# Unused matrix products of 64 columns in place of 128, in a kernel whose order is planned ahead

## The chip, the cores and the metric

The kernel runs on one core of one Trainium2 chip. The metric is device time in microseconds, the median of repeated executions; lower is better. A core has a matrix engine (PE, with its weight loads shown apart as PEld), two elementwise engines that read the matrix engine's results (DVE and ACT), a third that does not (POOL), and a queue that issues DMA transfers (SP).

## The reference

Attention over 4 batches, 8 heads, 576 tokens, 64 features a head, then two feed-forward layers over the 2304 tokens:

```python
scores = scale * np.matmul(q, k.transpose(0, 1, 3, 2))
thresh = np.max(scores, axis=-1, keepdims=True) - tau
scores = np.where(scores >= thresh, scores, -1000000000.0)
attn = softmax(scores);  x = np.matmul(attn, v)      # to [2304, 512]
h = x @ w_in                                          # 512 -> 2048
g = np.where(h >= 1, h, np.where(h <= -1, 0.0, (h + 1) ** 2 / 4))
x = g @ w_out                                         # 2048 -> 512
h = x @ w_in2;  r = np.maximum(h, 0.0)
out = (s * (r * r) + b) @ w_out2
```

All inputs and the result are float32.

## The kernel before, in words

Attention goes through 32 units (batch, half of the query rows, pair of heads). For a block of 128 query rows of a head, PE makes the scores (lines 583 and 592), DVE takes the row's extreme (line 638), ACT the exponentials (641), DVE masks and sums (646), one of three engines normalizes (676, 681), PE transposes the result (702, 718), ACT or DVE copies it out of the matrix engine's result banks (694), and PE multiplies it with the values (740, 741). Beside the first units, parts of the first feed-forward layer run (935 hidden products, 968 output products; 1016 is its remainder after attention). The other half of that layer and the second layer follow in three passes over three blocks of 768 tokens (lines 1230, 1270, 1306), with weights split into two parts and some products combined so that fewer are needed.

The order of the instructions on every engine is fixed when the program is written. Each step is a `Task` with a priority, the engines that could do it and a cost in nanoseconds; `Sched.run` simulates the engines with these costs and with fixed hand-over times between engines (`HOP`), and gives every free engine the ready task of the best priority. The instructions are then written in the order of the planned starts. Result banks are part of the plan: a task group gets a bank when one is free in the plan.

One rule concerns the matrix engine alone. Whenever it has nothing ready in the plan, before 200 us of planned time (`FILL`), and one of the banks 7, 6, 5, 4 is free, `Sched.run` puts in a product that nobody reads: `fill`, line 1406, identity times identity, written to that bank. In the plan it occupies the matrix engine for `fill_ns`, 213.0, plus a change cost between kinds of work (`CHANGE`), and holds the bank for that time; then the engine looks for ready work again. So a gap of the plan holds as many such products as are needed to cover it. The plan also models the matrix engine's clock (`Array`), in which these products count as work. Products planned before 4.5 us (`FILL_FROM`) are not written out. The program's warm-up (line 788) is five products of the same form.

Of the kernel before, what the change touches and what calls it, by code (L numbers as in the profile page):

```python
# [37 lines left out]
FILL = 200000.0  # L38
# [328 lines left out]
def attention_then_ffn(tc, qk, v, tau, w1, w2, s2, b2, out):  # L367
    nc = tc.nc
    sch = Sched()
# [18 lines left out]
    ident = lp.tile([128, 128], F32, name="ident")  # L388
# [51 lines left out]
    bank = [ps2[i][:, x, :] for i in range(2) for x in range(2)] + [t[:, :] for t in ps1] + [ps3[:, x, :] for x in range(2)]  # L440
# [962 lines left out]
        gemm2(P, t0, T)  # L1403

    def fill(b):
        return lambda: nc.tensor.matmul(bank[b][:, 0:128], ident, ident, start=True, stop=True)

    sch.fill_until, sch.fill_banks, sch.fill_ns, sch.fill = FILL, (7, 6, 5, 4), 213.0, fill
    order = sch.run()
    with tc.manual_schedule():  # L1410
        for t in order:
# [70 lines left out]
```

## Time and profile before

| | us |
|---|---|
| median of 3 runs | 1068.74 |
| lowest, highest | 1066.87, 1070.09 |
| the profiled execution, its own time | 1070.16 |
| its span, first to last instruction | 1068.4 |

| engine | busy us | share of the span | instructions |
|---|---|---|---|
| PE | 1044.9 | 98% | 6464 |
| PEld | 924.2 | 86% | 6464 |
| DVE | 802.4 | 75% | 1585 |
| ACT | 708.3 | 66% | 1325 |
| POOL | 434.5 | 41% | 660 |

Busy time is the time in which at least one instruction of the engine runs. Instructions of PE overlap, so a group's busy time is less than count times mean. An entry "idle before" is the time in which the engine did nothing ahead of an instruction, with the instruction that released it. PEclk is the granted share of the matrix engine's full clock of 2.4 GHz; 0.50 is 1.2 GHz.

### The profile page before, as it was taken

What the parts mean: (1) busy time and instruction counts of PE and PEld (TensorE: products, weight loads), DVE (VectorE), ACT (ScalarE), POOL (GpSimd) and SP (SyncE); (2) the same over time, 40 slices, a digit from 0 to 9 for tenths busy, and PEclk for the clock granted to TensorE, in tenths of its full rate; (3) what the DMA queues carried; (4) which work ended last, traced back from release to release, by engine and by line L of the source; (5) the groups of instructions that cost most, each with busy time, mean ns of one, the idle gap of its engine ahead of it and who ended that gap; (6) DMA issues with size and microseconds to landing.
All of it is one profiled execution on the core that took longest, in us unless ns stands there. A gap on an engine that the chain in (4) does not pass through costs nothing.

```text
span 1068.4 us, 19016 instructions
## 1 busy us (share of the span) xinstructions
PE 1044.9 (98%) x6464; PEld 924.2 (86%) x6464; DVE 802.4 (75%) x1585; ACT 708.3 (66%) x1325; POOL 434.5 (41%) x660
## 2 busy tenths in 40 slices
PE   8989999999999999999999999999999999999998
PEld 5556867788888988889999999998988989898996
DVE  7978998788787888857897988787696826446372
ACT  7988888989998988844544636367495735437260
POOL 5766767889798887623212202120111100010000
PEclk9989999999999999999999999999999999999999
DMA  5644465565656664599956579863539943230112
GB/s 179 197 145 145 141 185 186 182 183 172 189 158 213 189 207 155 172 313 373 350 173 218 167 255 387 295 221 138 174 112 306 373 140 118 77 101 20 60 30 89
DMA packets 105120, 199.95 MB, mean 187 GB/s; under 512 B 11328, under 2 KB 33344, under 8 KB 105024
## 3 DMA queue, kind: packets, MB, share of 16 engines
q1 hardware_dynamic: 105024, 198.75, 56.3%
q8 instruction: 51, 0.84, 0.3%
q14 instruction: 45, 0.37, 0.1%
HBM read 134.61 MB, written 64.09 MB: 186 GB/s over the span
## 4 chain that ended last, share of the span: by engine, by line
PE 71%; ACT 7%; DVE 5%; POOL 3%; issue 2%; DMA 1%; DVEq 0%; POOLq 0%; ACTq 0%; SPq 0%
PE ps L1230 24%; PE ps L1306 18%; PE ps L1270 9%; PE ps L935 5%; PE ps L968 4%; PE ps L702 2%; PE ps L740 2%; PE ps L1016 2%; ACT p L681 2%; PE ps L592 2%; DVE p L646 1%; ACT e L641 1%; ACT pt L694 1%; PE ps L583 1%; POOL lr L561 1%
## 5 line engine op out<-in xcount | busy, mean ns | idle before, releaser
L1230 PE MATMUL ps<-pr,lr 128*128 128x384 f32 x816 | 144.2, 334 | 0.0
L1230 PEld LDWEIGHTS ps<-pr,lr 128*128 128x128 f32 x816 | 141.6, 188 | 0.0
L646 DVE SCALAR_TENSOR_TENSOR p<-ps,stt,e 128x576 f32<-128x576 f32 x144 | 116.3, 812 | 22.9 <-ACT e L641 16.7
L1230 PE MATMUL ps<-lr 128*128 128x384 f32 x672 | 121.2, 334 | 0.1
L638 DVE TENSOR_REDUCE stt<-ps 128x1 f32<-128x576 f32 x144 | 105.8, 749 | 17.8 <-PE ps L592 9.3
L1230 PEld LDWEIGHTS ps<-lr 128*128 128x128 f32 x672 | 117.0, 188 | 0.9 <-DVE pf L1135 0.5
L935 PE MATMUL ps<-xh,lr 128*128 128x320 f32 (+1 forms) x512 | 112.5, 299 | 0.3 <-DVE lf L945 0.2
L641 ACT ACTIVATE e<-ps,stt 128x576 f32<-128x576 f32 x144 | 105.7, 749 | 8.6 <-DVE stt L638 8.1
L681 ACT ACTIVATE p<-p,stt 128x576 f32<-128x576 f32 (+3 forms) x112 | 93.2, 837 | 13.3 <-DVE stt L665 12.1
L562 DVE TENSOR_TENSOR pr<-lg,pr 128x768 fp32r<-128x768 f32 x71 | 70.9, 1004 | 39.5 <-POOL pr L845 25.9
L1306 PE MATMUL ps<-lr,pr 128*128 128x512 f32 x432 | 99.1, 390 | 0.0
L1306 PEld LDWEIGHTS ps<-lr,pr 128*128 128x128 f32 x432 | 81.0, 188 | 16.6
L1134 ACT COPY lg<-ps 128x384 f32<-128x384 f32 (+1 forms) x113 | 55.4, 493 | 60.3 <-PE ps L1230 41.6
L702 PE MATMUL ps<-ident,p 128*128 128x128 f32 x576 | 83.2, 276 | 7.5 <-ACT pt L694 5.3
L935 PEld LDWEIGHTS ps<-xh,lr 128*128 128x128 f32 x512 | 85.1, 188 | 3.2 <-DVE lf L945 0.9
L968 PE MATMUL ps<-g,lr 128*128 128x256 f32 (+1 forms) x600 | 87.2, 297 | 0.0
L1138 DVE TENSOR_TENSOR lg<-lg,ps 128x384 f32<-128x384 f32 (+1 forms) x104 | 57.2, 561 | 37.0 <-PE ps L1306 19.3
L702 PEld LDWEIGHTS ps<-ident,p 128*128 128x128 f32 x576 | 66.2, 141 | 20.3 <-ACT pt L694 5.9
L694 ACT COPY pt<-ps 128x512 f32<-128x512 f32 x143 | 79.8, 590 | 5.5 <-PE ps L702 5.1
L968 PEld LDWEIGHTS ps<-g,lr 128*128 128x128 f32 x600 | 80.7, 189 | 0.0
L935 PE MATMUL ps<-xl,lr 128*128 128x256 f32 (+1 forms) x256 | 75.3, 294 | 0.0
L845 POOL CAST pr<-lf 128x768 fp32r<-128x768 f32 x6 | 5.0, 831 | 166.8 <-PE ps L1306 116.6
(127 smaller groups left out, 2335.2 us busy)
## 6 DMA issues: line engine op xcount, KB each, us to landing
wd<-lh SPq DMA_DIRECT2D x118, 256.0 KB, 3.9
lr<-wd SPq DMA_DIRECT2D x108, 256.0 KB, 5.7
lk<-in_w_dram SPq DMA_DIRECT2D x48, 512.0 KB, 4.7
vr<-in_v_dram SPq DMA_DIRECT2D x32, 320.0 KB, 3.4
r<-in_qk_dram SPq DMA_DIRECT2D x32, 288.0 KB, 3.0
lg<-y1T SPq DMA_DIRECT2D x6, 1536.0 KB, 6.8
lk<-in_w_dram SPq DMA_DIRECT2D x32, 256.0 KB, 3.7
r<-in_qk_dram SPq DMA_DIRECT2D x16, 304.0 KB, 4.4
```

The source lines that it names most:

```text
L562: ("dve", dve_ns(n), lambda: nc.vector.tensor_tensor(out=o(), in0=x(), in1=y(), op=op), True)]
L638: add([("dve", 665, lambda: nc.vector.tensor_reduce(out=nm[:, x:x + 1], in_=Sv(), axis=AX.XY, op=ALU.min))], at(pr, "min"), r=[kg], w=[ks[ ...
L641: add([("act", 624, lambda: nc.scalar.activation(out=ev, in_=Sv(), func=AF.Exp, bias=nm[:, x:x + 1], scale=-1.0))], at(pr, "exp"), r=[kg, ...
L646: nc.vector.scalar_tensor_tensor(out=p[:, x * S:x * S + S].rearrange("p (a c) -> p a c", a=2), in0=Sv(), scalar=nthr[:, x:x + 1], in1=ev, ...
L681: nc.scalar.activation(out=p[i:j, o:o + w], in_=p[i:j, a:a + w], func=AF.Identity, scale=rc[i:j, x:x + 1], bias=un[i:j, x:x + 1])
L694: add([("act", actp_ns(n), lambda: [nc.scalar.copy(out=a, in_=b) for a, b in zip(dst, src())]), ("dve", dve_ns(n), lambda: [nc.vector.tens ...
L702: nc.tensor.transpose(bank[g.banks[0]][:, j * 128:(j + 1) * 128], p[:, c0 + j * 128:c0 + (j + 1) * 128], ident)
L935: nc.tensor.matmul(o, a, x, start=(n == 0), stop=(n == 11))
L968: nc.tensor.matmul(o, a[:, c], x, start=(f == 0 and n == 0), stop=(f == nf - 1 and n == 2))
L1230: nc.tensor.matmul(o, a, y, start=(i == 0 and p in (1, 5, 2)), stop=(i == 5), skip_group_check=p not in (1, 5, 2))
L1270: nc.tensor.matmul(o, w, x, start=(f == rows[0] and s == 0), stop=(f == rows[-1] and s == 2))
L1306: nc.tensor.matmul(o, a, y, start=(f == rows[0] and s == 0), stop=(f == rows[-1] and s == 2))
```

## The change

The unused product keeps its stationary operand, the whole 128x128 identity, and streams 64 columns of it in place of 128. Its planned cost is 107 ns in place of 213. As the planner uses this cost, it draws a new order for the whole program.

```diff
     def fill(b):
-        return lambda: nc.tensor.matmul(bank[b][:, 0:128], ident, ident, start=True, stop=True)
+        return lambda: nc.tensor.matmul(bank[b][:, 0:64], ident, ident[:, 0:64], start=True, stop=True)

-    sch.fill_until, sch.fill_banks, sch.fill_ns, sch.fill = FILL, (7, 6, 5, 4), 213.0, fill
+    sch.fill_until, sch.fill_banks, sch.fill_ns, sch.fill = FILL, (7, 6, 5, 4), 107.0, fill
```

## Rows read from the trace of the kernel before

**Rows 1.** The page, busy time of each engine.

```profile
PE 1044.9 (98%) x6464; PEld 924.2 (86%) x6464; DVE 802.4 (75%) x1585; ACT 708.3 (66%) x1325; POOL 434.5 (41%) x660
```

**Rows 2.** Stretches: start and end, length, busy us (instructions) of each engine, clock.

```profile
core 0: us, PE busy (x) PEld busy (x) DVE busy (x) ACT busy (x) POOL busy (x), PEclk, DMA share, GB/s
...
20.00:34.00 14.00, 13.80 (x95) 8.33 (x93) 13.32 (x39) 13.60 (x28) 9.00 (x20) 1.00 0.53 159
...
66.48:73.31 6.83, 6.62 (x28) 3.16 (x29) 4.79 (x13) 5.88 (x14) 2.63 (x7) 0.50 0.33 99
...
137.00:150.00 13.00, 12.69 (x98) 9.72 (x98) 12.70 (x37) 12.66 (x30) 7.04 (x15) 1.00 0.68 207
...
205.00:500.00 295.00, 287.14 (x2133) 257.57 (x2130) 233.35 (x542) 240.20 (x493) 221.55 (x309) 1.00 0.65 208
500.00:900.00 400.00, 399.61 (x2182) 382.11 (x2181) 307.07 (x472) 216.91 (x352) 61.67 (x66) 1.00 0.68 235
900.00:1066.50 166.50, 164.48 (x815) 147.16 (x814) 84.89 (x120) 73.48 (x106) 9.35 (x11) 1.00 0.18 60
```

**Rows 3.** Lines 1406 and 788: durations in ns (least/median/most), first and last start.

```profile
L1406 PEld LDWEIGHTS ps<-ident x94: 186/192/333, 5.2 to 149.4; 128*128 128x128 f32 x94
L1406 PE MATMUL ps<-ident x94: 272/275/579, 5.2 to 149.6; 128*128 128x128 f32 x94
...
L788 PE MATMUL ps<-ident x10: 421/421/582, 1.3 to 3.4; 128*128 128x128 f32 x10
```

**Rows 4.** Timeline from 4.9 to 12.7 us: start, length, engine, line, operation, count.

```profile
5.20 0.30 PEld L1406 LDWEIGHTS ps<-ident 128*128 128x128 f32 x2 [0.66 <-issue]
...
7.66 1.19 PEld L1406 LDWEIGHTS ps<-ident 128*128 128x128 f32 x10 [0.39 <-issue]
...
8.97 0.76 PE L583 MATMUL ps<-r 64*128 64x288 f32 x4
...
9.65 0.74 PEld L1406 LDWEIGHTS ps<-ident 128*128 128x128 f32 x6 [0.39 <-issue]
...
10.10 0.76 DVE L638 TENSOR_REDUCE stt<-ps 128x1 f32<-128x576 f32 x1
```

**Rows 5.** The chain of waits from 97 to 152 us: start, length, what.

```profile
100.22 0.71 PE ps L1406 x4
...
149.16 0.67 PE ps L1406 x6
```

**Rows 6.** Timeline of PE from 137 to 151 us.

```profile
138.16 0.49 PE L1406 MATMUL ps<-ident 128*128 128x128 f32 x2
...
140.03 0.39 PE L1406 MATMUL ps<-ident 128*128 128x128 f32 x2
```

**Rows 7.** Weight loads of 64 and of 128 columns, by line.

```profile
L740 PEld LDWEIGHTS ps<-pt,vr x512: 132/137/231, 20.1 to 457.9; 128*64 128x64 f32 x171
...
L592 PEld LDWEIGHTS ps<-lr x208: 186/188/249, 214.8 to 445.5; 128*128 128x128 f32 x104
```

**Rows 8.** PE's waits, 20 to 137 us: total us, times, longest.

```profile
PE ps L702 <- ACT pt L694: 2.2, 5, 1.0
PE ps L718 <- ACT pt L694: 1.4, 2, 0.8
PE ps L583 <- DVE p L646: 1.4, 2, 0.8
PE ps L1406 <- ACT lf L977: 0.6, 1, 0.6
PE ps L1406 <- ACT pt L694: 0.5, 1, 0.5
PE ps L702 <- ACT pl L694: 0.3, 1, 0.3
```

**Rows 9.** Timeline of PE from 55 to 76 us, before the clock fell.

```profile
64.41 1.09 PE L702 MATMUL ps<-ident,p 128*128 128x128 f32 x8 [1.00 <-ACT pt L694]
66.33 0.37 PE L718 MATMUL ps<-ident,p 128*128 128x128 f32 x1 [0.83 <-ACT pt L694]
```

## The prediction

> **What bounds the kernel now.** I read the page's totals first. PE is busy for 98% of the span and DVE for 75% [rows 1], but a share of the whole mixes stages, so the next view was the table of stretches. From 500 to 1066 us PE is idle for 2.4 us in all (0.39 and 2.02) and the other engines have room: that part is PE's own stream of products and the change has no instruction there [rows 2]. The first 200 us are different. DVE and ACT are nearly as full as PE (12.70 and 12.66 of 13.00 us between 137 and 150), PE runs out of ready work, and there the unused products stand: 94 instructions of line 1406 between 5.2 and 149.6 us [rows 2, 3]. The third view was the order in time of that part, the fourth the chain of waits.
>
> One planned product is two matmul instructions, each with its own weight load: the warm-up, written as five products of the same form, is ten [rows 3]. So the 94 are 47 products. In the timeline they stand in 23 runs: eleven of two instructions, four of four, five of six, two of eight, one of ten. After nearly all of them the real work follows without a wait, as at 8.97 us [rows 4]: the product of the plan was the last thing that the real work waited for. The chain of waits says the same for the late ones: from 100.22 to 149.83 us it runs through nine of these runs, 42 instructions, 5.4 us; the first and the last stand in [rows 5].
>
> **What one product costs on the chip.** The number of products is fixed when the order is written. In the plan a product of 128 columns costs 213 ns, one of 64 will cost 107. The trace has what 128 cost. The weight loads of a run of ten take 1.19 us and those of a run of six 0.74, so four more instructions take 0.45 us, 0.112 each. That is 224 ns a product beside 213 in the plan, a good price [rows 4].
>
> What sets this 0.112? Either the 128 columns that stream, or the weight load, which stays whole: the change cuts the moving operand, the stationary one is still the full 128x128 identity. The loads bear on it twice. Two loads of a run that starts on a resting array take 0.30 us together and one lasts 0.19 [rows 3], so the second starts 0.11 us after the first, when nothing had yet streamed [rows 4]. And a run of two that follows other work without a gap takes 0.39 us, one that starts after a gap 0.49: the load that nothing covered costs 0.10 [rows 6]. A load of 64 columns is 51 ns shorter in its record than one of 128 (medians 137 and 188 ns), which is again 0.10 for 128 columns [rows 7]. So the load of 128 columns occupies its path for 0.10 to 0.11 us, as long as the 128 columns of the product do. Halving the columns takes away one of two equal limits. I take 109 ns per instruction, 218 per product, twice the new price; the ends are 58 ns (columns alone: 112 less half of 107) and 112 (no gain).
>
> The Trainium skill speaks for both ends: "TensorE: Matmul & The Clock Gate", section "Back-to-back issue gap", gives the spacing from the streamed columns alone (56 ns at 128, about half at 64), and its section on LDWEIGHTS gives 107 ns for 128 stationary columns whatever streams. By the first a product would really halve, which is the third rival below; the trace's second load, 0.11 us after the first with nothing streaming, is with the second [rows 4].
>
> **The sum.** A gap of the plan that took k products of 213 ns takes 2k-1 or 2k of 107. With 2k less a half on average, 23 runs make 94 x 2 - 23 = 165 instructions.
> - Before: 94 x 0.112 = 10.5 us. After: 165 x 0.109 = 18.0 us. The last product of each run streams 53 ns less: 23 x 0.053 = 1.2 us back. Together +6.3 us on PE.
> - Ends: at 58 ns 165 x 0.058 - 10.5 = -0.9 us; at 112 ns with 2k everywhere 188 x 0.112 - 1.2 - 10.5 = +9.3 us.
> - How much reaches the end? Of the 94, 42 in nine runs lie on the chain [rows 5]. They become 75: 75 x 0.109 - 9 x 0.053 - 42 x 0.112 = +3.0 us, and I count it whole: PE was the last to arrive there, and from 150 us on PE has few waits that could take up a delay. The other 52 in 14 runs become 90: +3.2 us. For them there is cover. At 8.97 us the scores are done by 9.73 and DVE starts on them at 10.10 [rows 4], 0.37 us of slack, less than the 0.9 us by which the run of ten before them would grow. But PE itself waits 6.4 us for ACT and DVE between 20 and 137 us [rows 8], and a PE that comes later waits less. Bounds 0 and 3.2; I take 1.3. If the cover is gone, 1.9 us more.
> - The order drawn anew moves every other instruction as well. No row prices that. PE is idle 7.9 us of 205 to 500 [rows 2]; an order could win at most that or lose about as much. I take 0, and about 3 us either way for the range.
>
> Sum: 3.0 + 1.3 = +4.3 us. Against the profiled execution, 1070.2 us with 1.8 us outside its span of 1068.4, that is 1074.5. This execution lies 1.4 above the median 1068.7, so against the median the forecast is **1073.0 us**.
>
> **What else could happen.** About 0.3% (3.2 us) is what a measurement of this kernel can tell from no change: 1065.5 to 1072.0 counts as the same.
>
> *First, the clock falls more often: 1077 to 1080.* Once in the span the granted clock is at the lower level, 1.2 GHz, from 66.48 to 73.31 us [rows 2]. What PE did before was a few transposes between waits of 1.00 and 0.83 us for ACT [rows 8, 9]. Half speed over 6.83 us costs up to 3.4 us. The unused products are there to prevent this, and one of 64 columns streams 53 ns of 109 where the old one streamed nearly all the time; the plan counts both as full work. If one or two stretches (5 to 20, 137 to 150) fall because of it: 1073.0 + 3.4 = 1076.4, or + 6.8 = 1079.8. Against it: the runs are short and real products stand between them. Chance 0.15.
>
> *Second, the other side: PE's lateness removes its waits and with them the fall of the clock: 1065.* The overruns begin at 7.66 us, so PE comes later to the transposes for which it now waits 6.4 us between 20 and 137 [rows 8]. If all of these waits go, the bunch at 64.4 to 66.9 goes too, no lull stands at 66 us, and the clock stays at 2.4 GHz: 6.4 + 3.4 = 9.8 us won against 6.3 spent, -3.5 us, 1065.2. It decides the sign once waits and fall together give back over 6.3 us, and it beats the 0.3% only if nearly all of it comes. For it: ACT is 13.60 of 14.00 busy from 20 to 34 us, a queue that a later PE would find shorter. Against it: many of these waits are for an eviction of PE's own transposes, which come later with PE. With the freely drawn order, which could also lose the lull by itself, chance 0.21.
>
> *Third, the change does what its price says, and it does not matter: 1067 to 1069.* If the load were hidden and an instruction took 58 ns, PE would spend 0.9 us less on unused products, and real work would start up to half an old product earlier after each run, at most 23 x 0.053 = 1.2 us. Together -2.1 us, 1066.6, inside the noise. The same verdict comes if the gaps of the new order are few. Chance 0.20.
>
> **How the numbers follow.** The forecast has 0.44, with its own range 1070 to 1077 (the carried part between 1.3 and 8 us). Of it 0.34 lie above 1072.0 and 0.10 within. The falling clock gives 0.15 to slower. The second case gives 0.15 to faster, 0.06 to the same. The third 0.15 to the same, and the free order 0.03 to faster, 0.02 to slower. Faster 0.18, same 0.31, slower 0.51. The range 1065 to 1079 leaves out the case of two falls and an order better than the second case.
>
> **What would show it.** Line 1406 in the profile after: about 165 instructions (144 to 188), loads still 0.19 us long each, and a long run advancing 0.107 to 0.112 us an instruction. If a run advances by 0.06, the load step is wrong and the third case holds. The stretch from 97 to 151 us should be longer by about 3 us, most of it line 1406 on the chain of waits. From 500 us on the stretches should be equal to a microsecond. A second low stretch of the granted clock shows the first rival; none at all, with PE's waits between 20 and 137 us well under 6.4, the second. The prediction fails if the count of unused products stays near 94, or if it doubles and the end still doesn't move.

## The result, and the profile after

The change makes the kernel slower: 1080.13 us median (1068.46 to 1084.15, 13 runs) beside 1067.87 (1065.68 to 1070.26, 13 runs), ratio 1.0099, 95% interval 1.0079 to 1.0119. Ratios, here and below, are taken over the executions of both kernels and are not the quotient of the medians: this one stands for 10.6 us, while the medians differ by 12.3. The direction was forecast, but with 4.3 us; 1080.13 lies outside the range. The times after also scatter over 15.7 us where before they kept within 4.6. Two executions further down, 1154.65 us of warm_64_early and 1282.84 us of warm_small_load, had a mean granted clock of 0.85 and 0.75; the ratios leave them out, the medians count them.

The page of after, span and busy times, answers [rows 1]; the profiled execution took 1080.13 us, the median.

```profile
span 1078.3 us, 19091 instructions
## 1 busy us (share of the span) xinstructions
PE 1055.8 (98%) x6512; PEld 935.8 (87%) x6512; DVE 804.0 (75%) x1605; ACT 704.4 (65%) x1312; POOL 442.3 (41%) x653
```

Shares are nearly those of before. The stretches of after, cut as in [rows 2] (the last two lines come from answers with other cuts):

```profile
20.00:34.00 14.00, 13.90 (x77) 9.02 (x78) 9.73 (x26) 9.22 (x18) 7.25 (x19) 1.00 0.15 41
...
205.00:500.00 295.00, 290.96 (x2161) 257.86 (x2160) 235.28 (x558) 245.18 (x507) 233.96 (x326) 1.00 0.63 202
500.00:900.00 400.00, 400.00 (x2208) 382.58 (x2207) 310.10 (x483) 216.12 (x350) 79.16 (x75) 1.00 0.70 243
...
0.00:26.18 26.18, 24.07 (x95) 18.09 (x95) 9.34 (x24) 9.09 (x15) 6.68 (x22) 1.00 0.42 130
...
84.20:87.62 3.42, 3.42 (x17) 2.58 (x17) 2.69 (x8) 2.87 (x5) 2.82 (x7) 0.50 0.12 45
```

From 20 to 34 us DVE and ACT have 9.73 and 9.22 us of work where before they had 13.32 and 13.60: they are fed late. From 0 to 26.18 us PE is busy for 24.07 us, and yet gets through 95 instructions, where before it did 118 in its first 23:

```profile
0.00:23.00 23.00, 19.98 (x118) 12.91 (x118) 16.46 (x44) 16.05 (x30) 12.04 (x35) 1.00 0.56 172
```

The column of the clock says 1.00 in the first 26.18 us of after, which is wrong: the record of the clock begins with its first change, a rise at 26.18 us, and the view fills in the full clock ahead of it. The durations tell it, in the timeline of PE from 0 to 30 us:

```profile
4.08 1.33 PE L583 MATMUL ps<-r 64*128 64x288 f32 x4 [0.23 <-ACT r L520]
5.34 0.69 PE L1406 MATMUL ps<-ident 128*128 128x64 f32 x2
...
8.78 4.53 PE L1406 MATMUL ps<-ident 128*128 128x64 f32 x20
13.23 1.33 PE L583 MATMUL ps<-r 64*128 64x288 f32 x4
14.50 2.40 PE L1406 MATMUL ps<-ident 128*128 128x64 f32 x10
...
20.41 1.33 PE L583 MATMUL ps<-r 64*128 64x288 f32 x4
...
26.38 0.76 PE L583 MATMUL ps<-r 64*128 64x288 f32 x4
```

The same four score products take 1.33 us until 24 us and 0.76 at 26.38. An unused instruction advances by 0.21 us ((4.53 - 2.40) / 10), twice the 0.112 of [rows 4]. PE is at 1.2 GHz for its first 26 us; before, the record begins with a rise at 5.04 us. The mean granted clock of an execution, which is on record for every one of them, has the same gap: it counts only what follows the first entry. It is 0.998 for the profiled execution of after (1080.13 us) and 0.998 for the one execution of after that took 1068.46 us, within the range of before. Falls of the clock after the first rise do not tell these two apart; a start at 1.2 GHz would, though the faster one has no profile. The scores that start here at 20.41 start before at 11.85, one line of its timeline of PE from 0 to 30 us:

```profile
11.85 0.76 PE L583 MATMUL ps<-r 64*128 64x288 f32 x4
```

So 8.6 us are lost when the twenty-first score instruction starts. The chain of waits of after in that time runs through the unused products, which answers [rows 5]; two more long runs stand on it later (answers for 0 to 30 and 150 to 172 us):

```profile
8.85 4.46 PE ps L1406 x20
13.30 1.26 PE ps L583 x4
14.57 2.33 PE ps L1406 x10
...
154.35 1.51 PE ps L1406 x14
...
160.68 2.85 PE ps L1406 x26
```

At the other end the loss is already complete. The chain of before between 500 and 700 us, then that of after:

```profile
535.46 33.28 PE ps L1270 x192
568.74 29.12 PE ps L1230 x168
```

```profile
545.35 33.28 PE ps L1270 x192
578.63 29.12 PE ps L1230 x168
```

9.89 us later, the same lengths: the stream from 500 us on is untouched, as forecast. The two profiled executions differ by 9.97 us in all. Line 1406 in the trace after, against [rows 3, 7]:

```profile
L1406 PEld LDWEIGHTS ps<-ident x142: 186/192/333, 5.3 to 214.6; 128*128 128x128 f32 x142
L1406 PE MATMUL ps<-ident x142: 222/275/474, 5.3 to 214.7; 128*128 128x64 f32 x142
```

142 instructions where 94 were, each with the old load of 0.19 us. At the full clock the two runs of the chain, 26 and 14 instructions, differ by 1.34 us: 0.112 each. And PE's waits from 20 to 137 us, against [rows 8], have grown, first two lines of eight that sum to 10.9 us (1.6 of them for a DMA) beside 6.4:

```profile
PE ps L583 <- DVE p L646: 4.7, 5, 1.9
PE ps L718 <- ACT pt L694: 1.7, 2, 0.9
```

### The profile page after: what moved, and what is told of

The parts are those of the page before. It is cut to its first block, busy times and chain, and to the rows that moved or that the text cites. A ratio compares the mean times of both kernels' runs of the same rounds, so it can differ in the third digit from the quotient of the medians.

```text
span 1078.3 us, 19091 instructions
## 1 busy us (share of the span) xinstructions
PE 1055.8 (98%) x6512; PEld 935.8 (87%) x6512; DVE 804.0 (75%) x1605; ACT 704.4 (65%) x1312; POOL 442.3 (41%) x653
## 4 chain that ended last, share of the span: by engine, by line
PE 75%; ACT 9%; DVE 7%; POOL 4%; issue 3%; DMA 1%; SPq 0%; POOLq 0%; DVEq 0%; ACTq 0%
PE ps L1230 24%; PE ps L1306 18%; PE ps L1270 9%; PE ps L935 5%; PE ps L968 4%; PE ps L740 3%; ACT p L681 3%; DVE p L646 3%; PE ps L583 2%; PE ps L702 2%; ACT e L641 2%; PE ps L1016 2%; PE ps L1406 2%; ACT pt L694 2%; POOL lr L561 1%
## 5 line engine op out<-in xcount | busy, mean ns | idle before, releaser
L641 ACT ACTIVATE e<-ps,stt 128x576 f32<-128x576 f32 x144 | 105.7, 749 | 13.3 <-DVE stt L638 12.7
L681 ACT ACTIVATE p<-p,stt 128x576 f32<-128x576 f32 (+3 forms) x109 | 90.5, 832 | 12.1 <-DVE stt L665 10.3
L562 DVE TENSOR_TENSOR pr<-lg,pr 128x768 fp32r<-128x768 f32 x70 | 68.1, 973 | 40.3 <-POOL pr L845 25.5
L1134 ACT COPY lg<-ps 128x384 f32<-128x384 f32 (+1 forms) x108 | 52.8, 492 | 66.7 <-PE ps L1230 49.0
L740 PE MATMUL ps<-pt,vr 128*64 128x256 f32 (+1 forms) x512 | 69.8, 415 | 0.5 <-DVE lf L945 0.5
```

Of the source, the lines that this page charges most:

```text
L641: add([("act", 624, lambda: nc.scalar.activation(out=ev, in_=Sv(), func=AF.Exp, bias=nm[:, x:x + 1], scale=-1.0))], at(pr, "exp"), r=[kg, ...
L681: nc.scalar.activation(out=p[i:j, o:o + w], in_=p[i:j, a:a + w], func=AF.Identity, scale=rc[i:j, x:x + 1], bias=un[i:j, x:x + 1])
L740: nc.tensor.matmul(o[64 * x:64 * x + 64, 0:n], vr[:, c:c + D], PT[:, x, k, c0:c0 + n], start=(k == 0), stop=False)
```

## The experiments

Theory A: a product that loads 128 columns for 0.11 us and streams 64 for half of that leaves PE streaming half the time, and in most executions the clock then stays at 1.2 GHz through the first 26 us. Rival B: there are more products and each takes as long as ever. Rival C: the redrawn order. Each run has a profile of one execution; "first rise" is the first entry of its record of the clock, "score" the start of the twenty-first score instruction (line 583), which stood at 11.85 us before. The median of before is that of the same job, 1067.8 to 1069.1.

| kernel | first rise, us | score, us | median, us | ratio to before, 95% interval |
|---|---|---|---|---|
| before | 5.04 | 11.85 | 1067.87 | |
| after | 26.18 | 20.41 | 1080.13 | 1.0099 (1.0079 to 1.0119) |
| old_order_64 | 23.69 | 16.00 | 1071.25 | 1.0026 (1.0009 to 1.0042) |
| new_order_128 | 5.50 | 13.87 | 1070.84 | 1.0027 (1.0013 to 1.0041) |
| new_order_128_early | 12.55 | 17.23 | 1076.22 | 1.0077 (1.0061 to 1.0093) |
| new_order_64_early | 27.98 | 20.26 | 1079.37 | 1.0094 (1.0081 to 1.0107) |
| new_order_128_until_120 | 11.44 | 16.45 | 1073.62 | 1.0051 (1.0036 to 1.0066) |
| new_order_small_load | 10.07 | 13.37 | 1063.49 | 0.9959 (0.9943 to 0.9975) |
| old_order_small_load | 5.28 | 11.34 | 1066.55 | 0.9976 (0.9966 to 0.9986) |
| small_load_true_price | 9.32 | 12.75 | 1075.27 | 1.0059 (1.0047 to 1.0071) |
| small_load_stream_32 | 4.96 | 11.63 | 1072.14 | 1.0030 (1.0011 to 1.0049) |
| stream_32_long_warmup | 5.97 | 12.06 | 1066.32 | 0.9986 (0.9977 to 0.9996) |
| new_order_64_long_warmup | 7.11 | 14.97 | 1073.80 | 1.0042 (1.0026 to 1.0058) |
| warm_128_all | 6.03 | 14.65 | 1073.14 | 1.0045 (1.0033 to 1.0057) |
| warm_128_early | 5.14 | 14.28 | 1071.82 | 1.0034 (1.0017 to 1.0050) |
| warm_64_early | 4.95 | 13.96 | 1070.58 | 1.0025 (1.0013 to 1.0038) |
| warm_small_load | 7.49 | 12.86 | 1065.46 | 0.9978 (0.9964 to 0.9993) |

### Columns and order apart: old_order_64, new_order_128

```diff
 # old_order_64: the order of before, planned with 213.0
-        return lambda: nc.tensor.matmul(bank[b][:, 0:128], ident, ident, start=True, stop=True)
+        return lambda: nc.tensor.matmul(bank[b][:, 0:64], ident, ident[:, 0:64], start=True, stop=True)
 # new_order_128: the order of after, planned with 107.0
-        return lambda: nc.tensor.matmul(bank[b][:, 0:64], ident, ident[:, 0:64], start=True, stop=True)
+        return lambda: nc.tensor.matmul(bank[b][:, 0:128], ident, ident, start=True, stop=True)
```

> The order of before, instruction for instruction; only what the 47 unused products stream is 64 columns in place of 128. Theory A (late clock: products that stream half the time leave the matrix engine's clock at 1.2 GHz until about 26 us): the profile shows a first rise later than the 5.0 us of before in at least some runs, the times scatter as after's do (15 us from lowest to highest), the median is 3 to 8 us above before. Rival B (load-bound products: there are more of them and each takes 0.109 us an instruction, which is nearly what the old ones took): the count stays 94, so no change, 1066 to 1069, and as narrow as before. Rival C (the redrawn order itself): no change, since the order is the old one.

> The order of after, instruction for instruction; the 71 unused products stream 128 columns. A: the clock rises before 12 us, the 20th score product stands within 3 us of before's 11.85 us, the times are narrow again and the median is 1068 to 1074: what is left over before is the larger number of products. B: the products take as long as with 64 columns (0.112 against 0.109 us an instruction), so the time is after's, 1079 to 1082. C: the same, 1079 to 1082.

PE's timeline of old_order_64, a run of ten and the score, then of new_order_128, the run of twenty and the score:

```profile
8.64 2.39 PE L1406 MATMUL ps<-ident 128*128 128x64 f32 x10
...
16.00 1.33 PE L583 MATMUL ps<-r 64*128 64x288 f32 x4
```

```profile
7.44 2.50 PE L1406 MATMUL ps<-ident 128*128 128x128 f32 x20
...
13.87 0.76 PE L583 MATMUL ps<-r 64*128 64x288 f32 x4
```

With 64 columns the old order too runs its start at half speed, ten instructions in 2.39 us. With 128 the new order does twenty in 2.50. Given back their columns, the products of the new order take the ratio from 1.0099 to 1.0027: 0.72%, 7.7 us (0.5 to 1.0% by the two intervals), is what narrow products cost in this order, and B and C, which expected 1079 to 1082, have about 0.27%, 2.9 us (1.4 to 4.4), between them.

The traces say where. After and new_order_128 have the same 6512 instructions of PE in the same order, so each can be set against its counterpart. After's are 9.0 us behind from 18 to 51 us, 6.7 at 102, 7.8 from 223 on and 8.35 from 564 on: all of the loss is made in the start. Between 51 and 102 us after wins some back; there new_order_128 is the longer of the two at 1.2 GHz, for 13.65 us beside 3.42:

```profile
56.70:60.12 3.42, 3.27 (x18) 2.05 (x17) 2.59 (x8) 2.95 (x9) 2.20 (x7) 0.50 0.12 37
70.36:80.59 10.23, 9.58 (x40) 6.02 (x42) 8.15 (x26) 9.49 (x20) 6.64 (x15) 0.50 0.34 107
```

One line of new_order_128's chain between 500 and 700 us, against 545.35 of after:

```profile
537.00 33.28 PE ps L1270 x192
```

In the old order the same narrowing costs 0.26%, 2.3 us by the medians, less than A's 3 to 8 us, and the times scatter over 9.0 us where A expected 15: it has fewer such products at the start (28 instructions before 20 us in the trace of before, where the trace of after has 48 before 23), and the profiled execution lost 6.8 us by the first product with the values (26.85 us beside 20.07) but did not have the fall at 66.48 of [rows 2] and came out 2.3 us behind. A is right in kind here, its size only in part.

### What a short load is worth: new_order_small_load, old_order_small_load, small_load_true_price

```diff
-        return lambda: nc.tensor.matmul(bank[b][:, 0:64], ident, ident[:, 0:64], start=True, stop=True)
+        return lambda: nc.tensor.matmul(bank[b][0:64, 0:64], ident[:, 0:64], ident[:, 0:64], start=True, stop=True)
 # new_order_small_load: planned with 107.0; old_order_small_load: with 213.0; small_load_true_price: with 124.0
 # (the last two put the + line in place of before's line of 128 columns)
```

> The order of after; the unused products load 64 columns of the identity and stream 64, into 64 rows of the bank, so that neither load nor stream is long. Load step: at the full clock a run advances by 0.055 to 0.065 us an instruction, against 0.107 to 0.109 in after. A: PE streams nearly without a break in such a run, so the clock rises early and the median is 1064 to 1071; if it does not rise although a run advances by 0.06, it is not the share of time in which PE streams that matters. B: 142 x 0.05 = 7 us less work on PE, 1072 to 1075, and after's scatter. C: 1078 to 1082.

> The order of before, planned with 213; the 47 unused products load 64 columns and stream 64. 94 instructions of 0.062 in place of 0.112 us: 4.7 us less work on PE, 2.1 of it in the runs that lay on the chain of waits. If time on PE in these stretches is what an unused product costs: 1064 to 1067. If the gaps are set by other engines there and PE would only wait instead: 1068 to 1070. If the shorter products leave PE idle long enough for the clock to stay low: above 1070.

> Small products (64 loaded, 64 streamed) planned at 124 ns, which is what two instructions of 0.062 us take, so the order is drawn anew once more. If a price that agrees with the chip is what helps: at or below the 1063.5 of the same product priced 107, 1059 to 1064. If the drawing of the order is a matter of chance within some microseconds: 1060 to 1070 on either side.

PE's timeline of new_order_small_load from 0 to 30 us:

```profile
8.56 2.05 PE L1406 MATMUL ps<-ident 128*64 128x64 f32 x20
...
11.23 0.80 PE L1406 MATMUL ps<-ident 128*64 128x64 f32 x10
...
13.37 0.76 PE L583 MATMUL ps<-r 64*128 64x288 f32 x4
14.05 0.56 PE L1406 MATMUL ps<-ident 128*64 128x64 f32 x6
```

Ten take 0.80 us and six 0.56: 0.060 an instruction in place of 0.112, so the load was the limit. The kernel is faster than before and than new_order_128, 1063.49 us, just below the 1064 to 1071 that A expected. Against new_order_128, same order, it does 142 x (0.112 - 0.060) = 7.4 us less on PE, and its median is 7.35 us lower. That the two agree does not show that PE's time on unused products counts whole: of the 7.5 us between the two profiled executions 1.0 is there by 51 us, after 60 of the 142 instructions, and 5.3 come between 51 and 102 us, where 34 of them stand (1.8 us) and where new_order_128 has its 13.65 us at 1.2 GHz, the small load 3.41. In the old order 94 x 0.052 = 4.9 us gave 0.24%, 2.6 us, about half, within the 1064 to 1067 expected. The price 124 that fits these products drew a third order, 0.59% slower than before and 1.0% slower than the same product priced 107 (the expected 1060 to 1070 was too narrow). Part of it is lost late: PE idles 2.8 us between 460 and 575 in the first line, none in the matching stretch of new_order_small_load, which is the second line.

```profile
460.00:575.00 115.00, 112.22 (x715) 110.64 (x712) 88.38 (x143) 52.27 (x97) 38.62 (x34) 1.00 0.86 297
```

```profile
453.00:568.00 115.00, 115.00 (x735) 114.07 (x732) 88.43 (x152) 51.33 (x94) 21.62 (x27) 1.00 0.88 304
```

The cause of that in the plan stays open.

### Streamed share alone: small_load_stream_32, stream_32_long_warmup

```diff
-        return lambda: nc.tensor.matmul(bank[b][0:64, 0:64], ident[:, 0:64], ident[:, 0:64], start=True, stop=True)
+        return lambda: nc.tensor.matmul(bank[b][0:64, 0:32], ident[:, 0:64], ident[:, 0:32], start=True, stop=True)
 # stream_32_long_warmup, in the warm-up, with the plan unchanged
-            for _ in range(WARM):
+            for _ in range(2 * WARM):
```

> The order of after; the unused products load 64 columns and stream 32 into 64 rows. In the run before, with 64 loaded and 64 streamed, an instruction took 0.060 to 0.064 us and streamed most of that time. Here the load of 0.05 us sets the pace, 0.055 to 0.062 us, and the stream fills half of it. A (the share of time in which PE streams decides whether the clock rises): the rise in the profile comes after 15 us and the times scatter over 8 us or more, median 1066 to 1073. Rival D (what decides is how many instructions PE gets through, not how long they stream): the clock rises by 12 us, 1062 to 1065, as narrow as with 64 streamed.

> The kernel with 64 loaded and 32 streamed, whose runs fell into two groups (2 of 12 at 1065.4 to 1065.9, ten at 1071.2 to 1075.7; the profiled one was of the first group and its clock rose at 4.96 us). The warm-up is ten products of 128 columns in place of five, with the plan and the order unchanged. Price: at 1.2 GHz five more products take ten instructions of 0.23 us, the first scores start up to 2.0 us later. A (the two groups are runs whose clock rose before the unused products began, and runs whose clock did not): all runs in the first group, 1065 to 1069, spread under 4 us. Rival (the groups have another cause): still two groups, 1067 and 1073 to 1078.

PE's timeline of small_load_stream_32 around 7 to 13 us:

```profile
7.58 1.35 PE L1406 MATMUL ps<-ident 128*64 128x32 f32 x20
...
9.54 0.77 PE L1406 MATMUL ps<-ident 128*64 128x32 f32 x10
...
11.63 0.76 PE L583 MATMUL ps<-r 64*128 64x288 f32 x4
12.31 0.53 PE L1406 MATMUL ps<-ident 128*64 128x32 f32 x6
```

Order, number and pace (0.060) are those of new_order_small_load; only the stream is half as long. The ratio rises from 0.9959 to 1.0030, 0.71% or 7.6 us, and the runs fall into two groups, two at 1065.4 and 1065.9 and ten at 1071.2 to 1075.7. The profiled execution is one of the two: its clock rose at 4.96 us, ahead of the first unused product at 5.13, and its start is the fastest in the new order. A longer warm-up, which costs up to 2 us by itself, brings all nine runs to 1065.5 to 1068.9. Rival D, which expected 1062 to 1065 for any product of that pace, falls. That the first group is the one whose clock rises before the unused products is what A says of it; no execution of the second group was profiled. The recorded clocks speak for it: at the same mean of 0.995, which leaves the start out, two executions of the first group took 1065.36 and 1065.85 us, two of the second 1071.57 and 1071.67.

### The start or the rest: early, late and a longer warm-up

```diff
-                        t.fn = ("pe", self.fill_ns, self.fill(b))
+                        t.fn = ("pe", self.fill_ns, self.fill(b, now))
...
+        return lambda n=128 if now < 25000.0 else 64: nc.tensor.matmul(bank[b][:, 0:n], ident, ident[:, 0:n], start=True, stop=True)
 # new_order_64_early: 64 and 128 exchanged; new_order_128_until_120: 120000.0 for 25000.0
 # new_order_64_long_warmup: after, with range(2 * WARM) in the warm-up
 # warm_128_all, warm_128_early, warm_64_early: new_order_128 and the two mixtures, with range(2 * WARM)
```

> The order of after; unused products that the plan starts before 25 us stream 128 columns, the later ones 64. A: the whole difference to the run with 128 columns everywhere is small (under 2 us), the clock rises before 12 us: the loss is made in the first 26 us. If the clock falls again in later stretches, the time lies between that run and after's. B and C: 1079 to 1082.

> The order of after with the mixture turned round: products that the plan starts before 25 us stream 64 columns, the later ones 128. With 128 early and 64 late the ratio to before was 1.0077, with 128 everywhere 1.0027, with 64 everywhere 1.0099. If the loss were made by the late start of the clock alone (theory A in its strict form): 1.008 to 1.010 and times that scatter over 10 us. If early and late columns cost independently: 1.0099 less 1.0077 plus 1.0027, so about 1.005, 1073 to 1075. If only the late ones matter: 1.002 to 1.003.

> After, with ten products in the warm-up in place of five. A: the clock is up when the unused products begin and the start costs at most the 2 us of the longer warm-up, where it cost 8.6 us at the twentieth score product; the ratio falls from 1.0099 to that of the kernel with 128 columns early or below, 1.003 to 1.0077. Rival (the start is not the cause): 1.010 to 1.012.

> The order of after; products planned before 120 us stream 128 columns, the 46 instructions after that 64. With the border at 25 us the ratio was 1.0077, with 128 everywhere 1.0027. If the rest of the loss comes from falls of the clock between 56 and 118 us, which the profile of the run with the border at 25 us shows longer (17.1 us at 1.2 GHz against 13.7): 1.002 to 1.004. If it comes from the two long runs at 154 to 164 us: 1.006 to 1.008.

> The order of after, ten products in the warm-up, 128 columns in all unused products after it. With the clock up in every execution before the first of them, what is left over before is the longer warm-up (up to 2 us), the larger number of products and the redrawn order: ratio 1.001 to 1.004, narrow.

> As the run with 128 columns everywhere and the long warm-up, but 64 columns in the products planned after 25 us. If late narrow products cost by themselves (falls of the clock after 50 us): 0.002 to 0.005 above that run. If the 1.0077 of the same mixture with the short warm-up came from executions whose clock rose late: within 0.0015 of that run.

> As the run with 128 columns everywhere and the long warm-up, but 64 columns in the products planned before 25 us. The clock is up before they begin. If narrow products only fail to raise it: within 0.0015 of that run, where the same mixture with the short warm-up stood at 1.0094. If they also let it fall again between 7 and 26 us: 0.004 or more above it.

64 columns before 25 us alone give 1.0094 of 1.0099, the strict form of A, though its four executions kept within 2.8 us where A expected a scatter of 10. But 128 there and 64 later gave 1.0077, where A expected less than 2 us above new_order_128's 1.0027 or, if the clock fell again later, a time between the two, and with the border at 120 us 1.0051, between both expectations. The profiles offered a reason: in these two the clock rose at 12.55 and 11.44 us, with the same instructions up to there as in new_order_128, where it rose at 5.50. It is half of the reason: instruction for instruction, new_order_128_early is 3.4 us behind new_order_128 from 10 to 51 us and 6.9 from 564 us on. The rest came later, a part of it with falls of the clock after the first rise: its profile has 17.07 us of them beside 13.65, and five of its six executions have a mean granted clock of 0.992, where eight of the twelve of new_order_128 have 0.998. The timelines of new_order_128_early and of new_order_64_early show what a late rise is worth in the first run of twenty and at the score:

```profile
9.25 4.06 PE L1406 MATMUL ps<-ident 128*128 128x128 f32 x20
...
17.23 0.76 PE L583 MATMUL ps<-r 64*128 64x288 f32 x4
```

```profile
8.63 4.53 PE L1406 MATMUL ps<-ident 128*128 128x64 f32 x20
...
20.26 1.33 PE L583 MATMUL ps<-r 64*128 64x288 f32 x4
```

So the three warm runs took the luck of the start away with the longer warm-up; in their profiles the clock rises at 4.95 to 6.03 us, before the first unused product at 6.16 to 6.64. 128 everywhere stands at 1.0045 (1.001 to 1.004 was expected), 64 late at 1.0034, 64 early at 1.0025 (0.0020 below the first, where 0.0015 either way was expected). The narrow ones are not slower, and the intervals overlap. After itself goes from 1.0099 to 1.0042 with ten warm-up products, and at the score its profile is 0.3 us behind that of warm_128_all, where after was 6.5 behind new_order_128. So in these runs no cost of 64 columns is left once the clock is up before the first unused product, and the rival "late narrow products cost by themselves" finds no support.

What is left is scatter, and it goes with the falls after the first rise: in warm_128_early the five executions with a mean granted clock of 0.998 took 1068.0 to 1069.2 us, the five with 0.991 to 0.994 took 1073.6 to 1075.6. These falls need no narrow products: all five executions of warm_128_all have 0.993 to 0.995. Differences of 0.3% between kernels of this order can therefore be a matter of which executions were drawn.

A last run, warm_small_load, was new_order_small_load with the longer warm-up:

> The fastest kernel so far (64 loaded, 64 streamed, the order of after, ratio 0.9959) with ten products in the warm-up. In its profile the clock rose at 10.07 us; the longer warm-up costs up to 2 us and wins what the late rise cost, about 1.5 us at the twentieth score product: 0.995 to 0.998.

It reached 1065.46, ratio 0.9978 (0.9964 to 0.9993), at the upper end of what was expected and not below the 0.9959 without: no gain from a longer warm-up is seen for that product.

## Why the prediction was wrong

- **The clock** is the step that failed. The sum put it at nothing; it stands as the first rival, at 0.15, as stretches that fall once the clock is up. By its sign, a second low stretch in the record, that rival did not come: after has one, half as long as before's. The runs show another form of it: in the profiles of kernels with narrow products and a whole load the clock rises only at 23.69 to 27.98 us, after nearly all the unused products of the start. Narrow in place of wide costs 0.72%, 7.7 us, in the same order, more than all the rest, and in the traces 9.0 us by 18 us. The working had the fact that does it (53 ns of streaming in 109) and set it aside with "the runs are short and real products stand between them". It also counted one low stretch in the span of before, though the record begins only at 5.04 us and says nothing of what came ahead of it. The forecast of 4.3 with 7.7 added would have been 12.0; measured were 10.6 by the ratio, 12.3 by the medians.
- **The load step** was right: 0.112 us an instruction, 0.060 with half the load. The Trainium skill, "TensorE: Matmul & The Clock Gate", section on LDWEIGHTS, times a load by its own columns, and the trace agrees (0.19 us records, 0.112 us apart, at 128 columns streamed as at 64); the spacing by streamed columns alone, which the page's section "Back-to-back issue gap" gives for an isolated matmul, does not hold here.
- **The count** was 142, just below the 144 to 188 given. The order of after gathers them in fewer and longer runs, 18 in place of some 23. At 0.112 us 48 more instructions are 5.4 us on PE, 4.2 after the 1.2 that the sum takes off, in place of the forecast 6.3.
- **What of it reaches the end**: forecast 4.3 us. new_order_128, which has the count and the order but not the columns, is 0.27%, 2.9 us (1.4 to 4.4), behind before. The forecast lies inside that interval, but the agreement is luck in part: the products of the new order stand at 9 to 23, 99 to 102 and 154 to 164 us, not where the sum had them, and new_order_128 is also at 1.2 GHz for 13.65 us where before is for 6.83. One execution of after took 1068.46 us, 0.6 above before's median. How much the larger number costs by itself stays open. The sign set for 97 to 151 us cannot be read, as the new order does other work there.
- **The redrawn order** was taken as 0 with 3 us either way. Two drawings with the same product, priced 107 and 124, lie 1.0%, 10.7 us, apart (1.0059 and 0.9959). For this planner 3 us was too little. The order of after is not a bad one by itself: with the small load it is not behind the old order (0.9959 beside 0.9976).
- **The second rival** (fewer waits, no fall) did not come: waits of 10.9 us in place of 6.4, and a fall at 84.20, though one of 3.42 us in place of 6.83. **The third** needed 0.06 an instruction; that came only with the short load, and then it mattered.

## What to carry to other kernels

Before you shorten a filler that is meant to hold the matrix engine's clock up, ask which of its operands sets its pace. Here the whole load did: with half the columns streamed the fillers occupied the engine as long as before, and in the profiled executions the clock stayed at 1.2 GHz beside them. Cutting both operands to 64 columns made the filler short, and this kernel was the fastest of all (0.9959); with its stream halved again ten executions of twelve were slower than all of its own. Measure the drawing of the order apart from the filler. Where the first record of the clock is late, read the clock from the durations of equal instructions; and where two runs have the same order, set instruction against instruction to see where the time is lost.

## What was not expected of the hardware

- The first rise differs between profiled executions with the same instructions up to it: 5.50, 11.44 and 12.55 us with 128 columns. With 64 columns and a whole load it came at 23.69, 26.18 and 27.98.
- PE had an instruction in flight for 24.07 of the first 26.18 us of after and stayed at 1.2 GHz. The busy time of the profile, which counts an instruction's wait for its load, did not tell which clock was granted. With the small load and half the stream (small_load_stream_32) ten runs of twelve lay in the slower group; with the same pace and the full stream the six runs kept within 3.7 us.
- A fall in the middle of attention needs no narrow products: new_order_128 was at 1.2 GHz from 56.70 to 60.12 and from 70.36 to 80.59 us.
